# A pair's weighted sums, memory transposes and the second scores of the pair two later as one run of matmuls

## The chip, the cores and the metric

The kernel runs on one core of a Trainium2 chip. The metric is the device time of one execution in microseconds (us); of several executions the median counts. PE is TensorE, DVE VectorE, ACT ScalarE, POOL GpSimd, SP the engine that issues the loads.

## What is computed

An attention over 4 x 8 heads of 576 positions, 64 wide, with a recurrent memory mixed in, and two MLP layers on its output (512 to 2048 to 512 features, 2304 tokens):

```python
scores = scale * np.matmul(q, k.transpose(0, 1, 3, 2))
scores = np.where(causal, -1000000000.0, scores)
a = softmax(scores)
local = np.matmul(a, v)
q_p = phi(q)                      # elu(q) + 1
mem_out = einsum(q_p, M_prev) / (einsum(q_p, z_prev) + 1e-06)
x = g * mem_out + (1 - g) * local
h = x @ w_in;  x = (h * sigmoid(1.702 * h)) @ w_out          # layer 0
h = x @ w_in2; x = (h * clip(h + 3, 0, 6) / 6) @ w_out2      # layer 1
```

## The kernel before

**Tiles and pairs.** The tokens are cut into 6 tiles of 384. A tile needs the attention of one query block of 384 rows (g == 0) or of two blocks of 192 (g == 1), and the 8 heads of a block are handled as 4 pairs: 32 pairs, 4 of them for the first tile, then 4, 8, 4, 4 and 8. While the MLP's layer 0 runs on one tile, the attention of the next tile is worked in between its matmuls. Only the first tile's four pairs come before all MLP work (the opening). Layer 1 has no attention beside it.

**Steps of a pair.** `scores` multiplies q and k in two products (L545 to L560): the first, and the second, which for g == 0 is the last query rows and for g == 1 the remaining 64 rows of both heads. After each come a masked row minimum on DVE (L484), the exponential on ACT (L489), a reciprocal on DVE and the scaling on POOL (L497). `turn` transposes the probabilities on PE (L439) and copies them out of PSUM (L584 or L586). `mem_read` multiplies phi(q) with the memory (L409) and DVE scales the result (L680). `weigh` multiplies the transposed probabilities with v into one bank o, and adds the transposed memory output to it by matmuls with an identity (L704, L717, all recorded at L424); ACT copies o to the MLP's input (L735). A matmul in plain f32 stands in the trace as two records.

**Order.** The generator `attention` works on three pairs at a time (L756 to L777): the scores of pair i, the transposes of pair i - 1, the sums of pair i - 2. Its steps are: first scores, first transposes, sums, second scores, second transposes, and so on; each `yield` gives control back to the MLP's stream, and `pump` (L826) takes so many steps for each quarter of an MLP unit. A planner then orders each engine's instructions by its own estimate of times: those that are ready, earliest in program order first. `issue_after` (L340) keeps the MLP from running more than `SLACK` = 10 attention steps ahead.

**Runs.** `in_a_run` (L419) makes a matmul function of which each call must come after the one before it on PE, without a semaphore; only the first matmul waits, for the instructions in `deps`. The order is fixed by it, but not that nothing else may come between.

**Banks.** `bank` (L382) hands out PSUM banks in turn: 8 in the opening, then the three of `psa`, while the MLP has the other five. `free(t)` names the instruction that last read the bank that t takes over. The sums' run before is `in_a_run(list(made.pop(i).values()))`, where `made` has the copies of the transposes and the scaled memory output; the wait for the bank o is added by the framework. The second scores have a run of their own, `in_a_run(free(banks[0]) + free(banks[1]))`.

Of the kernel before, what the change touches and what calls it, by code (L numbers as in the profile page):

```python
# [104 lines left out]
def attention_moe_kernel(ctx: ExitStack, tc: tile.TileContext, qk0, sk0, sk1, vm0, vm1, bb, w1, w2, out):  # L105
# [271 lines left out]
    banks = [3, 0, 0]  # L377
# [22 lines left out]
    def free(t):  # L400

        d = last_read.get(place[id(t)][0])
        return [] if d is None else [d]

    on_pe = []
# [10 lines left out]
                reason="one run of matmuls",  # L416
            )

    def in_a_run(deps):  # L419

        run = []

        def mm(out, **args):
            ins = PE.matmul(out, **args).ins  # L424
            if run:
                tc.add_manual_dep(
                    ins, run[-1].name,
                    mybir.DependencyInfo(mybir.DependencyClass.NoSync, mybir.DependencyReason.DATA),
                    reason="one run of matmuls",
                )  # L430
            else:
                after(ins, deps)
            run.append(ins)
            on_pe[:] = [ins]

        return mm
# [4 lines left out]
    def attention(ap):  # L441
        qk, vm, pp, pt, phi, mo = {}, {}, {}, {}, {}, {}
        gens, made = {}, {}
        norms = [0, 0]

        t4 = ap.tile([128, 2, 64], F32, tag="t4", bufs=1, name="t4")
# [5 lines left out]
        def need(*keys):  # L452
            for key in keys:
                gen = gens.pop(key, None)
                if gen is not None:
                    chains.finish(gen)
# [45 lines left out]
        def scores(i):  # L502

            ti, si, b, g, p, _ = pairs[i]
            norms[1] = ti
            q, k = qk[i]
            st = ap.tile([128, 12], F32, tag="st", name="st")
            mx, su = st[:, 0:6], st[:, 6:12]

            def product(banks, blocks):  # L510

                mm = in_a_run(free(banks[0]) + free(banks[1]))
                for o0, o1, c0 in blocks:
                    for a in range(2):
                        h = slice(64 * a, 64 * a + 64)
                        mm(
                            banks[a][:, o0:o1], lhsT=q[h, c0:c0 + 128], rhs=k[h, 0:o1 - o0], start=True, stop=True
                        )

            def soft(s, cols, dst, c):  # L520

                jobs = [(a, c0, c1, c + a * len(cols) + x) for a in range(2) for x, (c0, c1) in enumerate(cols)]
                yield
                for a, c0, c1, k in jobs:
                    masked_min(s[a][:, c0:c1], mask[:, 512 - (c1 - c0):512], BIG, mx[:, k:k + 1])
                yield
                for a, c0, c1, k in jobs:
                    d = expo(dst[a][:, c0:c1], s[a][:, c0:c1], mx[:, k:k + 1], su[:, k:k + 1])
                    if c1 == cols[-1][1]:
                        has_read(s[a], d)  # L530
                yield
                inverse(su[:, c:c + len(jobs)])
                yield
                for a, c0, c1, k in jobs:
                    norm(dst[a][:, c0:c1], su[:, k:k + 1], omg[:, 2 * p + a:2 * p + a + 1])

            pp[i] = []
            if g == 0:
                parts = (((0, 128, 0), (128, 384, 128)), ((0, 384, 256),))
            else:  # L540
                parts = (((0, 512, 0),),)
            t = [[ap.tile([128, 512], F32, tag="p", bufs=PB, name="p") for _ in parts] for _ in range(2)]
            pp[i] = [tuple(x) for x in t]
            c = 0
            for x, blocks in enumerate(parts):  # L545
                s = [bank("s") for _ in range(2)]
                product(s, blocks)
                start(("s", i, x), soft(s, [(o0, o1) for o0, o1, _ in blocks], [t[a][x] for a in range(2)], c))
                c += 2 * len(blocks)
                yield  # L550
            if g == 1:
                t = ap.tile([128, 512], F32, tag="p", bufs=PB, name="p4")
                t2 = ap.tile([128, 64], F32, tag="p5", name="p5")
                pp[i].append((t, t2))
                s, s2 = bank("s4"), bank("s5")
                mm = in_a_run(free(s) + free(s2))
                for o, c0, c1 in ((s, 0, 512), (s2[:, 0:64], 512, 576)):
                    for a in range(2):
                        h = slice(64 * a, 64 * a + 64)
                        mm(o[h], lhsT=q[h, 128:N1], rhs=k[h, c0:c1], start=True, stop=True)  # L560

                def soft4(s=s, s2=s2, t=t, t2=t2):
                    yield
                    masked_min(s, mask[:, 0:1].to_broadcast([128, 512]), BIG, mx[:, 2:3])
                    masked_min(s2[:, 0:64], mask4, mx[:, 2:3], mx[:, 3:4])
                    yield
                    has_read(s, expo(t, s, mx[:, 3:4], su[:, 2:3]))
                    has_read(s2, expo(t2, s2[:, 0:64], mx[:, 3:4], su[:, 3:4]))
                    yield
                    DVE.tensor_tensor(out=su[:, 2:3], in0=su[:, 2:3], in1=su[:, 3:4], op=ALU.add)  # L570
                    inverse(su[:, 2:3])
                    yield
                    norm(t, su[:, 2:3], omp[:, p:p + 1])
                    norm(t2, su[:, 2:3], omp[:, p:p + 1])

                start(("s", i, 2), soft4())
                yield
# [114 lines left out]
        def weigh(i):  # L692

            ti, si, b, g, p, last = pairs[i]
            v = vm.pop(i)[0]
            t = pt.pop(i)
            need(("t", i, 0, 0), ("t", i, 0, 1), ("t", i, 1, 0), ("t", i, 1, 1), ("m", i))
            o = bank("o")
            mm = in_a_run(list(made.pop(i).values()))

            def av(j, rhs, c0, c1, first):
                for a in range(2):
# [33 lines left out]
                has_read(o, d)  # L736

            start(("x", i), split())
            yield

        def chunks(gen, n):
            for _ in range(n):
# [13 lines left out]
        for i in range(NPAIR + 2):  # L756
            if has(i):
                gs[i] = scores(i)
            if has(i - 1):
                gt[i - 1] = turn(i - 1)  # L760
            if has(i - 2):
                gw[i - 2] = weigh(i - 2)
            s, t, w = gs.pop(i, nil), gt.pop(i - 1, nil), gw.pop(i - 2, nil)
            for gen, n in (
                (s, 1), (t, 1), (w, 1), (s, 1), (t, 1), (w, 9), (s, 1), (t, 1), (s, 9),
            ):
                yield from chunks(gen, n)
            if has(i):
                start(("p", i), mem_prep(i))
                load_qk(i + 2)  # L770
            if has(i - 2) and pairs[i - 2][5]:
                need(("x", i - 2))
                yield pairs[i - 2][0]
            load_vm(i)
            if has(i - 1):
                yield from mem_read(i - 1)
            yield from chunks(t, 9)  # L777
# [180 lines left out]
```

## Time and profile before

| | us |
|---|---|
| median of 3 runs | 1064.96 (1061.93 to 1065.06) |
| profiled execution | 1062.62 |
| its span, first to last instruction | 1060.80 |
| mean granted TensorE clock | 0.995 |
| idle in the span: PE | 26.7 |

The page gives for each engine the busy time and its share of the span; the stretches give the same for parts of the span; the waits say who stood for whom; the timeline gives single instructions with their starts. Matmuls overlap, so the duration of one says less than the distance between two starts.

### The profile page before, as it was taken

To read this page: it belongs to the slowest core of one execution; us is meant where nothing else is said; L and a number is where in the kernel's file an instruction comes from. 1 tells how busy PE (TensorE), PEld (TensorE's weight loads), DVE (VectorE), ACT (ScalarE), POOL (GpSimd) and SP (SyncE) were. 2 spreads that over 40 slices of the span, in tenths; PEclk is the share of its full clock that TensorE was granted. 3 is DMA by queue.
4 is the path that set the end of the run, shared out by engine and by line. 5 is a ranking of instruction groups with operands and counts; after the bars stand their busy time and mean duration, and the time that the engine had idled before them with its cause. 6 is when DMAs were issued, how large, how long until landed. Compare 5 with 4: busy or idle time off the path is not lost.

```text
span 1060.8 us, 16126 instructions
## 1 busy us (share of the span) xinstructions
PE 1034.1 (97%) x6025; PEld 913.4 (86%) x6025; DVE 468.0 (44%) x1153; ACT 510.3 (48%) x1110; POOL 296.3 (28%) x346
## 2 busy tenths in 40 slices
PE   7899899999999999999999998999999999999998
PEld 4555456988788888888889998999999999999998
DVE  6975866666533333433344597881121111211210
ACT  5965745545544453433333677883233232332322
POOL 3511212323333232222322240432222222222221
PEclk9999999999999999999999999999999999999999
DMA  6753423332211111111100685001000010000000
GB/s 239 254 193 105 164 65 135 115 109 91 70 35 51 26 55 53 34 31 60 35 28 16 252 305 198 1 1 60 1 30 31 1 60 1 30 31 1 31 1 30
DMA packets 33886, 80.29 MB, mean 76 GB/s; under 512 B 4112, under 2 KB 13328, under 8 KB 33808
## 3 DMA queue, kind: packets, MB, share of 16 engines
q1 hardware_dynamic: 33808, 79.25, 22.3%
q8 instruction: 48, 0.79, 0.3%
q14 instruction: 30, 0.25, 0.1%
HBM read 61.41 MB, written 9.44 MB: 67 GB/s over the span
## 4 chain that ended last, share of the span: by engine, by line
PE 87%; ACT 5%; DVE 4%; DMA 3%; issue 1%; SPq 0%; POOL 0%; ACTq 0%; DVEq 0%; POOLq 0%
PE y L315 12%; PE y L317 11%; PE h L344 11%; PE y L316 11%; PE h L346 11%; PE h L347 11%; PE o L424 5%; PE s L424 5%; PE t L439 3%; PE y L313 2%; PE h L342 2%; ACT p L489 1%; PE mem L409 1%; DMA wt<-r 1%; ACT r L195 1%
## 5 line engine op out<-in xcount | busy, mean ns | idle before, releaser
L295 POOL TENSOR_TENSOR g<-t,g 128x384 fp32r<-128x384 f32 x173 | 186.5, 1079 | 482.1 <-ACT g L292 462.0
L344 PE MATMUL h<-xs,w 128*128 128x384 f32 x704 | 242.2, 344 | 6.0 <-DVE t L287 4.0
L315 PE MATMUL y<-g,w 128*128 128x384 f32 x704 | 237.6, 338 | 0.5 <-ACT g L292 0.5
L347 PE MATMUL h<-xs,w 128*128 128x384 f32 x704 | 236.7, 337 | 0.0
L316 PE MATMUL y<-g,w 128*128 128x384 f32 x704 | 236.6, 336 | 0.0
L346 PE MATMUL h<-xs,w 128*128 128x384 f32 x704 | 236.4, 336 | 0.0
L317 PE MATMUL y<-g,w 128*128 128x384 f32 x704 | 224.8, 338 | 0.0
L287 DVE SCALAR_TENSOR_TENSOR t<-t,h 128x384 f32<-128x384 f32 x96 | 53.1, 553 | 275.8 <-ACT t L285 275.6
L344 PEld LDWEIGHTS h<-xs,w 128*128 128x128 f32 x704 | 132.8, 189 | 13.9 <-issue 4.7
L497 POOL TENSOR_SCALAR p<-p,st,omg 128x128 f32<-128x128 f32 (+3 forms) x128 | 86.3, 686 | 199.8 <-DVE st L493 153.8
L285 ACT ACTIVATE t<-h,three 128x384 f32<-128x384 f32 x96 | 55.5, 579 | 173.4 <-PE h L347 172.1
L315 PEld LDWEIGHTS y<-g,w 128*128 128x128 f32 x704 | 132.2, 188 | 3.8 <-issue 1.0
L317 PEld LDWEIGHTS y<-g,w 128*128 128x128 f32 x704 | 130.5, 188 | 4.8 <-issue 4.1
L292 ACT CAST g<-t 128x384 fp32r<-128x384 f32 x176 | 90.1, 513 | 91.4 <-DVE t L287 49.3
L347 PEld LDWEIGHTS h<-xs,w 128*128 128x128 f32 x704 | 132.6, 188 | 0.5 <-issue 0.5
L346 PEld LDWEIGHTS h<-xs,w 128*128 128x128 f32 x704 | 132.9, 189 | 0.0
L316 PEld LDWEIGHTS y<-g,w 128*128 128x128 f32 x704 | 132.3, 188 | 0.5 <-issue 0.5
L489 ACT ACTIVATE p<-s,st 128x256 f32<-128x256 f32 (+4 forms) x160 | 82.4, 523 | 79.5 <-DVE st L484 63.5
L484 DVE CUSTOM_DVE_ANT_0 s<-s,mask 128x128 f32<-128x128 f32 (+3 forms) x144 | 72.2, 530 | 72.3 <-PE s L424 71.5
L281 ACT ACTIVATE t<-h 128x384 f32<-128x384 f32 x96 | 46.7, 489 | 73.0 <-PE h L347 54.3
L283 DVE SCALAR_TENSOR_TENSOR t<-t,h 128x384 f32<-128x384 f32 x80 | 44.0, 552 | 67.6 <-ACT t L281 60.5
L424 PE MATMUL s<-qk 64*128 64x256 f32 (+5 forms) x384 | 70.9, 460 | 2.2 <-ACT p L489 1.6
(82 smaller groups left out, 1110.5 us busy)
## 6 DMA issues: line engine op xcount, KB each, us to landing
r<-in_w_dram SPq DMA_DIRECT2D x64, 512.0 KB, 6.0
wt<-r SPq DMA_DIRECT2D x32, 256.0 KB, 2.4
vm<-in_vm_dram SPq DMA_DIRECT2D x16, 386.0 KB, 3.0
qk<-in_qk_dram SPq DMA_DIRECT2D x16, 384.0 KB, 3.7
qk<-in_sk_dram SPq DMA_DIRECT2D x32, 192.0 KB, 3.3
x2d<-yo SPq DMA_DIRECT2D x24, 192.0 KB, 2.0
xr<-x2d SPq DMA_DIRECT2D x24, 192.0 KB, 3.2
out_dram<-yo SPq DMA_DIRECT2D x24, 192.0 KB, 1.9
```

The source lines that it names most:

```text
L292: gated["ACT"].append(ACT.copy(out=g[:, 0], in_=t).ins)
L295: d = {"DVE": DVE, "POOL": POOL}[e].tensor_tensor(out=g[:, 1], in0=t, in1=f32(g[:, 0]), op=ALU.subtract)
L315: PE.matmul(ys[d], lhsT=w[:, 0, o:o + 128], rhs=g[:, 0], start=(f == 0), stop=False)
L316: PE.matmul(ys[d], lhsT=w[:, 1, o:o + 128], rhs=g[:, 0], start=False, stop=False)
L317: PE.matmul(ys[d], lhsT=w[:, 0, o:o + 128], rhs=g[:, 1], start=False, stop=(f == NF - 1))
L344: PE.matmul(h, lhsT=w[:, 0, c:c + 128], rhs=x[:, 0], start=first, stop=False)
L346: PE.matmul(h, lhsT=w[:, 1, c:c + 128], rhs=x[:, 0], start=False, stop=False)
L347: PE.matmul(h, lhsT=w[:, 0, c:c + 128], rhs=x[:, 1], start=False, stop=last)
L424: ins = PE.matmul(out, **args).ins
L484: DVE.tensor_tensor_reduce(out=o, in0=o, in1=m, scale=-SCALE, scalar=init, op0=ALU.add, op1=ALU.min, accum_out=out)
L489: return ACT.activation(out=dst, in_=o, func=AF.Exp, scale=-1.0, bias=m, accum_out=s)
L497: (DVE, POOL)[e[norms[0] % len(e)]].tensor_scalar(out=dst, in0=dst, scalar1=s, scalar2=w, op0=ALU.mult, op1=ALU.mult)
```

## The change

`weigh` now takes the two banks for the second scores of pair i + 2 first, and its own bank o after them; its first matmul waits for the copies, the memory output and the last readers of those two banks. It yields no longer in the middle: it leaves its last matmul in `tail`, and the second scores of pair i + 2, which are issued right behind it in the same step, take the two banks from `later` and put themselves behind `tail` without a wait of their own. One step with nothing in it (`yield None`) keeps the count of steps. The first scores are as before, as are the second scores of the first two pairs, and the sums of the last two pairs stand alone.

```diff
--- before.py
+++ after.py
@@ -416,9 +416,10 @@
                 reason="one run of matmuls",
             )
 
-    def in_a_run(deps):
-
-        run = []
+    def in_a_run(deps, run=()):
+
+
+        run = list(run)
 
         def mm(out, **args):
             ins = PE.matmul(out, **args).ins
@@ -441,6 +442,7 @@
     def attention(ap):
         qk, vm, pp, pt, phi, mo = {}, {}, {}, {}, {}, {}
         gens, made = {}, {}
+        later, tail = {}, []
         norms = [0, 0]
 
         t4 = ap.tile([128, 2, 64], F32, tag="t4", bufs=1, name="t4")
@@ -507,9 +509,17 @@
             st = ap.tile([128, 12], F32, tag="st", name="st")
             mx, su = st[:, 0:6], st[:, 6:12]
 
-            def product(banks, blocks):
-
-                mm = in_a_run(free(banks[0]) + free(banks[1]))
+            def two_banks(x):
+
+                s, run = later.pop((i, x), None), list(tail)
+                tail.clear()
+                if s is not None:
+                    return s, in_a_run([], run)
+                s = [bank("s") for _ in range(2)]
+                return s, in_a_run(free(s[0]) + free(s[1]))
+
+            def product(mm, banks, blocks):
+
                 for o0, o1, c0 in blocks:
                     for a in range(2):
                         h = slice(64 * a, 64 * a + 64)
@@ -543,8 +553,8 @@
             pp[i] = [tuple(x) for x in t]
             c = 0
             for x, blocks in enumerate(parts):
-                s = [bank("s") for _ in range(2)]
-                product(s, blocks)
+                s, mm = two_banks(x)
+                product(mm, s, blocks)
                 start(("s", i, x), soft(s, [(o0, o1) for o0, o1, _ in blocks], [t[a][x] for a in range(2)], c))
                 c += 2 * len(blocks)
                 yield
@@ -552,8 +562,7 @@
                 t = ap.tile([128, 512], F32, tag="p", bufs=PB, name="p4")
                 t2 = ap.tile([128, 64], F32, tag="p5", name="p5")
                 pp[i].append((t, t2))
-                s, s2 = bank("s4"), bank("s5")
-                mm = in_a_run(free(s) + free(s2))
+                (s, s2), mm = two_banks(1)
                 for o, c0, c1 in ((s, 0, 512), (s2[:, 0:64], 512, 576)):
                     for a in range(2):
                         h = slice(64 * a, 64 * a + 64)
@@ -692,11 +701,16 @@
         def weigh(i):
 
             ti, si, b, g, p, last = pairs[i]
+            yield from ()
             v = vm.pop(i)[0]
             t = pt.pop(i)
             need(("t", i, 0, 0), ("t", i, 0, 1), ("t", i, 1, 0), ("t", i, 1, 1), ("m", i))
+            deps = list(made.pop(i).values())
+            if has(i + 2):
+                later[i + 2, 1] = s = [bank("s") for _ in range(2)]
+                deps += free(s[0]) + free(s[1])
             o = bank("o")
-            mm = in_a_run(list(made.pop(i).values()))
+            mm = in_a_run(deps)
 
             def av(j, rhs, c0, c1, first):
                 for a in range(2):
@@ -736,7 +750,8 @@
                 has_read(o, d)
 
             start(("x", i), split())
-            yield
+            if has(i + 2):
+                tail[:] = on_pe
 
         def chunks(gen, n):
             for _ in range(n):
@@ -761,10 +776,16 @@
             if has(i - 2):
                 gw[i - 2] = weigh(i - 2)
             s, t, w = gs.pop(i, nil), gt.pop(i - 1, nil), gw.pop(i - 2, nil)
-            for gen, n in (
-                (s, 1), (t, 1), (w, 1), (s, 1), (t, 1), (w, 9), (s, 1), (t, 1), (s, 9),
-            ):
-                yield from chunks(gen, n)
+            yield from chunks(s, 1)
+            yield from chunks(t, 1)
+            for _ in w:
+                pass
+            if has(i - 2):
+                yield from chunks(s, 1)
+                yield None
+            yield from chunks(s, 1)
+            yield from chunks(t, 1)
+            yield from chunks(s, 9)
             if has(i):
                 start(("p", i), mem_prep(i))
                 load_qk(i + 2)
```

## Rows read from the trace of the kernel before

**Rows 1.** The page, part 1: busy us (share of the span) x instructions
```profile
PE 1034.1 (97%) x6025; PEld 913.4 (86%) x6025; DVE 468.0 (44%) x1153; ACT 510.3 (48%) x1110; POOL 296.3 (28%) x346
```

**Rows 2.** Stretches: length, busy us of each engine, granted clock, DMA share, GB/s
```profile
46.00:152.00 106.00, 100.35 (x417) 57.66 (x417) 75.32 (x158) 65.80 (x118) 25.60 (x26) 0.98 0.42 143
152.00:586.00 434.00, 429.54 (x2704) 366.31 (x2701) 200.19 (x619) 197.45 (x522) 128.83 (x166) 1.00 0.20 61
```

**Rows 3.** Waits of PE: who for whom, us in total, times, longest
```profile
PE o L424 <- ACT p L489: 2.6, 2, 2.1
```

**Rows 4.** PE's timeline at two pairs: start us, us, engine line op out<-in shape xcount
```profile
220.59 0.33 PE L316 MATMUL y<-g,w 128*128 128x384 f32 x1
...
221.28 0.34 PE L317 MATMUL y<-g,w 128*128 128x384 f32 x1
221.55 1.52 PE L424 MATMUL o<-pt,vm 128*64 128x192 f32 x16
...
223.49 1.19 PE L424 MATMUL s<-qk 64*64 64x512 f32 x8
...
224.89 0.34 PE L316 MATMUL y<-g,w 128*128 128x384 f32 x1
...
543.64 0.34 PE L315 MATMUL y<-g,w 128*128 128x384 f32 x1
543.90 1.52 PE L424 MATMUL o<-pt,vm 128*64 128x192 f32 x16
...
545.92 0.34 PE L317 MATMUL y<-g,w 128*128 128x384 f32 x1
...
546.27 0.34 PE L316 MATMUL y<-g,w 128*128 128x384 f32 x1
547.94 0.34 PE L344 MATMUL h<-xs,w 128*128 128x384 f32 x1
```

**Rows 5.** PE's timeline at a pair that was cut
```profile
483.34 0.34 PE L347 MATMUL h<-xs,w 128*128 128x384 f32 x1
483.61 1.19 PE L424 MATMUL o<-pt,vm 128*64 128x192 f32 x10
...
494.04 1.18 PE L424 MATMUL s<-qk 64*64 64x512 f32 x6
...
495.82 0.34 PE L346 MATMUL h<-xs,w 128*128 128x384 f32 x1
```

**Rows 6.** Timeline of all engines at three pairs; in brackets idle before and releaser
```profile
122.46 2.17 PE L424 MATMUL o<-pt,vm 128*64 128x384 f32 x12 [2.12 <-ACT p L489]
...
123.41 0.70 ACT L489 ACTIVATE p<-s,st 128x512 f32<-128x512 f32 x1
123.60 0.68 DVE L586 COPY pt<-t 128x512 f32<-128x512 f32 x1
...
198.98 1.52 PE L424 MATMUL o<-pt,vm 128*64 128x192 f32 x16
...
200.70 0.68 DVE L586 COPY pt<-t 128x512 f32<-128x512 f32 x1
...
237.38 1.52 PE L424 MATMUL o<-pt,vm 128*64 128x192 f32 x16 [0.50 <-ACT p L489]
237.60 0.69 ACT L489 ACTIVATE p<-s,st 128x512 f32<-128x512 f32 x1
```

**Rows 7.** PE's timeline in the opening
```profile
25.66 0.92 PE L424 MATMUL s<-qk 64*128 64x384 f32 x4
...
28.83 1.52 PE L424 MATMUL o<-pt,vm 128*64 128x384 f32 x12 [0.37 <-DVE mo L680]
...
44.28 0.94 PE L409 MATMUL mem<-vm,phi 128*128 128x130 f32 x6 [1.05 <-ACT p L489]
...
46.35 0.91 PE L342 MATMUL h<-x,r 128*128 128x384 f32 x2 [0.20 <-ACT pt L584]
```

**Rows 8.** A stretch around the stand at 122 us, columns as in the second group
```profile
122.00:128.00 6.00, 5.54 (x22) 3.36 (x23) 5.93 (x10) 2.68 (x6) 2.11 (x2) 0.72 0.31 98
```

## The prediction

> **What bounds the kernel now.** I read the page's busy line first, then the stretches, then TensorE's (PE's) waits, then its timeline around single pairs. PE is busy 1034.1 of 1060.8 us [rows 1], so time is saved only by taking work or idle time off PE. The change touches the attention, which PE runs up to 586 us, between the MLP's matmuls. By stretches PE stands idle 5.65 us from 46 to 152 us and 4.46 us from 152 to 586 us (length less busy time) [rows 2]. In the waits, the weighted sums stand for softmax exponentials 2.6 us in all, 2 times, the longest 2.1 [rows 3]. So waits in front of these sums are rare now, and idle time is no large store to win from. What is left is what it costs PE to turn from MLP matmuls to attention matmuls and back.
>
> **What a joined run saves.** There are 30 pairs whose sums are followed by scores of a later pair; 4 of them lie in the opening (before 46 us) and 26 later. First the step of the MLP's stream: four starts from 220.59 to 221.28 us, 0.173 us each [rows 4]. I price a visit to the attention by starts: from the start of the last MLP matmul before it to the second start after it, less two steps of 0.173 (the second, since the first one after a visit is drawn out). Apart, at 543.90 us: the 20 sums with their 2 transposes take 545.92 - 543.64 - 0.35 = 1.93 us, the 8 second scores 547.94 - 546.27 - 0.35 = 1.32 us, together 3.25 us. Joined, at 221.55 us, sums, transposes and scores in one go: 224.89 - 221.28 - 0.35 = 3.26 us [rows 4]. So a joined visit costs the same as two. PE already ran them joined in 21 of the 26 later pairs (the one of 221.55 among them), and the other 5 would gain nothing by it. Saved: 5 x -0.01 to 0.01 us, **0.0 us**.
>
> **What cuts cost, and whether the change mends them.** The links between a run's matmuls fix their order and no more: an MLP matmul may still be put between two of them. At 483.61 us the sums were cut after 10 of 20, and the scores ended at 494.04 with the 6 left over. From 483.34 to 495.82 us are 12.48 us; in them lie 38 MLP starts (6.57 us) and the 4 transposes of another product (0.44 us), which leaves 5.5 us for what costs 3.26 us uncut: 2.2 us lost [rows 5]. One other pair, of 174.62 us, is cut in its scores, by my reading of the same timeline for about 1.3 us, what the first piece of two matmuls costs alone (as many as eight cost together). So cuts that touch these runs cost 3.5 us. The scores are now issued one step earlier, together with the sums, and stand ahead of more MLP matmuls; that speaks for fewer cuts. But the sums were linked before too, and were cut. Bounds: -3.5 us (all mended) to +3 us (as many new ones); I take **-1.0 us**, a bit nearer to none, since the cause (an MLP matmul that comes due in mid-run) is not removed.
>
> **What the joined wait costs.** Before, the first sum waits for the evacuated transposes, the scaled memory output and one bank: of three attention banks it reuses the one that the first score product's first head left. The second scores wait, behind 1.9 us of sums, for the second head's exponential and for the evacuation of the transposes issued just before. After, the scores take their two banks first and the sums the third, and all of it is waited for in front of the first sum: both exponentials and that evacuation. A waiting sum holds the whole in-order PE, the MLP matmuls behind it, and through them the gates on ScalarE and VectorE. I go by each pair's rows and ask when the latest of the three was done. In 20 of the 26 later pairs all were done before the sums began; cost nothing, hidden by the MLP matmuls in front. Two pairs are the dear ones because PE already stands there: at 122.46 us the sums begin 0.15 us after one exponential, while the second ends at 124.11 and the copy at 124.28: 1.8 us more; at 237.38 us the second exponential ends at 238.29: 0.9 us more [rows 6]. In the other four the copy ends about when the sums begin or up to 2.4 us after it (the longest: sums at 198.98, copy done at 201.38 [rows 6]); there PE was not standing, MLP matmuls came next, and the scheduler, which places a run when its estimate says that it is ready, can put them in front. So between 0 (all covered) and 1.8 + 0.9 + 2.4 + 0.4 + 0.2 = 5.7 us (none covered); I take **+1.5 us**, about half of the two sure ones, since matmuls of the MLP follow them also. What comes next is later too: the next transposes now reuse a bank of the second scores and wait for its exponential, where they waited for the copy of the sums. Between visits lie MLP matmuls that cover it, as with the 20 pairs: 0, and where that cover is gone it is part of the slower rival.
>
> **The opening.** Here no MLP matmul covers anything. The second scores of pair 3 ran at 25.66 us, ahead of the sums of pair 1 at 28.83, which waited 0.37 us for the memory output [rows 7]. Bound to come after these sums, their 0.85 us leave a stretch in which PE idles anyway and move into one in which it runs densely: +0.85 us. Those of pairs 4 and 5 likewise change places with sums, inside dense work: 0 each. Against that, VectorE has one 0.55 us score mask less ahead of that memory output: down to -0.5 us. At the end, the memory product at 44.28 us waits 1.05 us for an exponential of pair 5's second scores, and the first MLP matmul follows at 46.35 us [rows 7]; with these scores later that wait may grow by the 1.5 us of the sums that now come first, or vanish, since the first MLP matmul can be put ahead. From -0.5 to +2.4 us; I take **+0.9 us**. The softmax of the second scores starts one step earlier, and nothing else moves: SP's loads and POOL's scaling keep their places in the generators' order.
>
> **Sum.** 0.0 - 1.0 + 1.5 + 0.9 = +1.4 us. The profiled execution took 1062.62 us (span 1060.80), so by itself 1064.0; the median of the three runs, 1064.96, is 2.3 us above it, so I forecast 1064.96 + 1.4 = **1066 us**, which is no change.
>
> **The rivals.**
> *Slower: the joined wait stands uncovered.* Place: the first sum of a pair. Price: 5.7 us of waits. To it comes the clock: from 122 to 128 us, after PE had stood 2.1 us and twice about 1 us before, the granted clock was 0.72 on average [rows 8], between its levels of 2.4 and 1.2 GHz; 6 x 0.28 = 1.7 us lost. With the opening's 0.9 and no mended cut that is +8.3 us: 1073 us. It decides from 3.2 us of new standing in front of the sums. For it: the two pairs of [rows 6]. Against it: the 20 pairs that have slack. The Trainium skill, "TensorE: Matmul & The Clock Gate", section "HAM oscillation — how this bites in real kernels", says that waits between bursts throttle the clock, so that the next burst runs cold; the trace agrees at 122 us (0.72) and nowhere else between 46 and 586 us. By that rule, one more such stand would cost another 1.7 us.
>
> *Faster: the cuts go, and so does the stand at 122 us.* Mended cuts give -3.5 us; a new order in which MLP matmuls stand before those sums gives the 2.1 us of waiting and the 1.7 us of clock back; -7.3 us at most, and with the opening's 0.9 about 1059 us, half of it 1062. For it: earlier scores, and a schedule that is made anew throughout. Against it: nothing in the change points at 122 us in particular, where it adds a wait.
>
> *It doesn't do what it says.* The run is only linked, and gets cut between sums and scores as before. A cut between the transposes and the scores costs nothing (1.93 + 1.32 against 3.26); one inside costs about 1.3 us. With four of these more, less the gain taken, it is 1064.96 + 0.9 + 1.5 + 3 = 1070 us; with none, the forecast.
>
> **How the numbers follow.** About 0.3% (3.2 us) is what a measurement of this kernel can tell from no change. Forecast 0.42 (within); slower by the uncovered wait 0.24; faster 0.26; cut as before 0.08, half of it within and half slower. So faster 0.26, within 0.46, slower 0.28. Cases of both signs hold more than half, so the forecast's own range stands apart: 1062 to 1069 us. The range of all reaches to the middle of the faster rival and to most of the slower one: 1059.5 to 1072 us.
>
> **What would show it.** Right: sums, transposes and scores without an MLP matmul between them in nearly all pairs, and a visit at 3.25 us; the span within 3 us. The waits of the sums for exponentials and copies then come to 3 to 5 us against 2.6 [rows 3]. The slower rival would show as such waits of over 6 us, or as a second stretch with the clock under 1; the faster one as idle time from 46 to 586 us well under 10.1 us, or no cut run. The opening is read off the first MLP matmul: 46.35 us now, 47.2 by the forecast. I am wrong in mechanism if a joined visit costs clearly less than 3.25 us, or if the time moves beyond 586 us, where nothing was changed.

## The result and the profile after

| | before | after |
|---|---|---|
| median (range) of five executions each, us | 1063.42 (1061.93 to 1065.06) | 1071.21 (1069.53 to 1074.77) |
| profiled execution, us | 1062.62 | 1069.53 |
| its span, us | 1060.8 | 1067.7 |

The changed kernel is slower by 0.8%: the ratio of the times is 1.0080, 95% interval 1.0065 to 1.0095. The time lies inside the stated range of 1059.5 to 1072 us, close to the upper end that the slower rival had set; the forecast itself, no change, did not come true.

First the page's busy line of the changed kernel, to be held against [rows 1]:

```profile
PE 1035.9 (97%) x6025; PEld 916.7 (86%) x6025; DVE 466.0 (44%) x1153; ACT 510.0 (48%) x1110; POOL 294.0 (28%) x346
```

The instructions are the same in number. PE is busy 1.8 us longer in a span that is 6.9 us longer, so it also stands idle 5 us more. The stretches (columns as in [rows 2]) say where:

```profile
0.00:46.00 46.00, 35.58 (x212) 23.40 (x214) 34.41 (x134) 32.41 (x101) 20.46 (x43) 0.93 0.64 229
46.00:152.00 106.00, 97.08 (x406) 55.61 (x402) 71.33 (x156) 66.97 (x120) 23.35 (x26) 0.97 0.41 143
152.00:586.00 434.00, 428.93 (x2688) 364.79 (x2685) 203.86 (x624) 197.95 (x528) 128.76 (x167) 1.00 0.19 61
```

From 46 to 152 us the idle time went from 5.65 to 106.00 - 97.08 = 8.92 us; from 152 to 586 us from 4.46 to 5.07 us. For a full account I split the span of the profiled executions into three parts: time in which no matmul record lies (idle), busy time times one less the granted clock (clock), and the rest, which is the work at full clock. Before: 26.8 + 5.1 + 1029.0. After: 31.8 + 8.9 + 1027.0. So 5.1 us more idle, 3.8 us more at the low clock, and 2.0 us less work. These are single executions; the changed kernel's is the fastest of its five.

The start of the first matmul of a tile gives the loss by place:

| profiled execution, us | first MLP matmul | second tile | sixth tile | end of span |
|---|---|---|---|---|
| before | 46.4 | 169.8 | 580.5 | 1060.8 |
| after | 42.7 | 176.7 | 587.0 | 1067.7 |

The changed kernel is 6.9 us late at the second tile, 6.5 us late at the sixth, and 6.9 us at the end. So the loss is there by the time the attention of the first 170 us is done. By the second tile both kernels have the same matmuls behind them, the sums of nine pairs among them, so the stretch from there to the sixth tile compares like with like: 410.8 us before and 410.3 after, with 1.6 us more idle time and 2.1 us less work.

PE's waits (engine, line, for whom; us in total, times, longest) of after, those that answer to [rows 3]:

```profile
PE s L425 <- ACT p L491: 5.4, 3, 2.0
PE mem L409 <- ACT p L491: 4.5, 4, 1.5
PE h L342 <- DVE r L206: 3.6, 1, 3.6
PE o L425 <- ACT p L491: 2.6, 2, 2.0
```

The sums' own waits for exponentials (the last line) are 2.6 us, as before. What grew stands in front of other work: first scores (s), memory products (mem), and one MLP matmul (h) that waits for a converted weight.

The largest of these stands, in the timeline of DVE and PE:

```profile
120.56 0.29 DVE L486 CUSTOM_DVE_ANT_0 s<-s,mask,st 128x64 f32<-128x64 f32 x1
...
120.77 0.69 DVE L186 TENSOR_SCALAR r<-r 128x1024 int32<-128x1024 int32 x1
...
123.92 1.22 PE L425 MATMUL s<-qk 64*128 64x512 f32 x4 [1.20 <-ACT pt L593]
...
128.06 1.22 DVE L206 SCALAR_TENSOR_TENSOR r<-r 128x1024 f32<-128x1024 f32 x1
...
129.33 2.93 PE L342 MATMUL h<-x,r 128*128 128x384 f32 x4 [3.61 <-DVE r L206]
```

and the stretch that begins in it (columns as in [rows 2]; the granted clock is ahead of the last two):

```profile
128.00:134.00 6.00, 4.67 (x8) 2.52 (x8) 3.52 (x8) 2.42 (x5) 1.51 (x2) 0.50 0.53 164
```

The MLP matmul at 129.33 us needs a weight whose conversion starts on DVE at 120.77 us, right behind the masks of second scores, and those are now behind the sums. It ends at 129.28 us, PE stands 3.61 us, and the granted clock from 128 to 134 us is 0.50, the lower of its two levels.

In the opening, PE's timeline, to be held against [rows 7]:

```profile
32.34 1.65 PE L425 MATMUL s<-qk 64*128 64x128 f32 x8 [1.87 <-ACT p L491]
...
41.39 0.93 PE L425 MATMUL s<-qk 64*128 64x128 f32 x8 [1.48 <-ACT p L491]
42.25 0.44 PE L440 MATMUL t<-ident,p 128*128 128x128 f32 x2
42.69 2.20 PE L342 MATMUL h<-x,r 128*128 128x384 f32 x6
44.82 1.41 PE L425 MATMUL o<-pt,vm 128*64 128x384 f32 x10
```

The first scores of pairs 4 and 5 stand 1.87 and 1.48 us for exponentials: by the order in which banks are handed out they take a bank of the second scores of pairs 3 and 4, and those run later now. The first MLP matmuls moved ahead of pair 3's sums, to 42.69 us.

### The profile page after: what moved, and what is told of

It is laid out like the page before. It is cut to its first block, busy times and chain, and to the rows that moved or that the text cites. A ratio compares the mean times of both kernels' runs of the same rounds, so it can differ in the third digit from the quotient of the medians.

```text
span 1067.7 us, 16107 instructions
## 1 busy us (share of the span) xinstructions
PE 1035.9 (97%) x6025; PEld 916.7 (86%) x6025; DVE 466.0 (44%) x1153; ACT 510.0 (48%) x1110; POOL 294.0 (28%) x346
## 4 chain that ended last, share of the span: by engine, by line
PE 89%; ACT 4%; DVE 4%; DMA 2%; issue 1%; SPq 0%; DVEq 0%; ACTq 0%
PE y L315 11%; PE h L344 11%; PE y L316 11%; PE y L317 11%; PE h L346 11%; PE h L347 11%; PE o L425 5%; PE s L425 5%; PE h L342 4%; PE y L313 3%; PE t L440 3%; ACT p L491 2%; PE mem L409 1%; DVE s L486 1%; DVE r L186 1%
## 5 line engine op out<-in xcount | busy, mean ns | idle before, releaser
L486 DVE CUSTOM_DVE_ANT_0 s<-s,mask 128x128 f32<-128x128 f32 (+2 forms) x144 | 72.3, 529 | 79.4 <-PE s L425 78.5
```

What stands on the lines that cost most here:

```text
L486: DVE.tensor_tensor_reduce(out=o, in0=o, in1=m, scale=-SCALE, scalar=init, op0=ALU.add, op1=ALU.min, accum_out=out)
```

## The experiments

Each was timed beside the kernel before on the same chip; that kernel's median was 1062.7 us in the first four runs that follow (e1 to e4), 1063.28 in the next four, and 1063.2 in the last four. Differences between two of these kernels are given below as differences of medians; by their ratios to the kernel before they come out within 0.7 us of that.

### Which half: the opening or the rest

**e1_late** joins from pair 4 on alone; **e2_opening** in pairs 0 to 3 alone. The edit is the same condition with the two signs:

```diff
-            if has(i + 2):
+            if joins(i):
                 later[i + 2, 1] = s = [bank("s") for _ in range(2)]
...
+        def joins(i):
+            return has(i + 2) and i >= 4
```

> Joined runs only from pair 6's second scores on (the sums of pairs 4 and later); the opening is as before. Theory O (opening): the whole loss comes from the opening, where sums and scores change places and banks, and from what follows from it up to 170 us; then the first MLP matmul starts at 46.4 us as before, no MLP matmul stands for a converted weight (3.6 us at 129 us in the changed kernel), tile 1 begins at 170 and the time is 1063 to 1065 us. Theory W (wait): the loss comes from the joined waits in front of the later pairs' sums; 26 of 30 joined runs are still there, so 1070 to 1072 us.

> The other half: joined runs only for the four sums of the opening (pairs 0 to 3), all later ones as before. Theory O: 1069 to 1072 us, tile 1 begins 6 to 7 us later than before (170). Theory W: 1063 to 1065 us. If both halves give about half of the 8 us, both hold.

Measured: e1_late 1069.52 us (1069.11 to 1071.19), ratio 1.0061 [1.0043, 1.0080]; e2_opening 1065.06 us (1062.63 to 1068.26), ratio 1.0022 [1.0008, 1.0036]. The two add up to 0.83%, the whole 0.80%. So about 2.4 us come from the opening and the larger part, some 6.8 us, from the pairs worked in between MLP matmuls. (e1_late is half a microsecond under theory W's range, e2_opening at the top of it. Theory O is out, though one of its signs holds for e1_late too: an MLP matmul stands for a converted weight, 2.22 us at 100 us.)

### The order of the banks

**e3_obank** is the changed kernel with the sums' bank taken first again:

```diff
+            o = bank("o")
             if has(i + 2):
                 later[i + 2, 1] = s = [bank("s") for _ in range(2)]
                 deps += free(s[0]) + free(s[1])
-            o = bank("o")
```

**e7_swapbanks** is the kernel before with that order alone changed, and no run joined:

```diff
+            if has(i + 2):
+                later[i + 2, 1] = [bank("s") for _ in range(2)]
             o = bank("o")
```

> The changed kernel with one thing undone: the sums take their bank first and the second scores the next two, as before; the runs stay joined, and the first sum still waits for all three. Theory O by banks: in the opening the first scores of pairs 4 and 5 no longer take over a bank of the second scores just before them (they stood 1.9 and 1.5 us for its exponential), so half or more of the 8 us comes back: 1064 to 1067 us. Theory O by order (the second scores stand behind the sums whatever the bank): 1069 to 1072. Theory W: the waits are the same three, 1070 to 1072 us.

> The kernel before with one thing changed: the second scores' two banks are taken ahead of the sums' bank. Undoing the banks' order in the changed kernel gave nothing (1071.0), so 1061 to 1065 us; if the order costs by itself in the opening (first scores that take over a bank of second scores), 1065 to 1067.

Measured: e3_obank 1070.97 us, ratio 1.0069 [1.0048, 1.0090], not apart from the changed kernel; e7_swapbanks 1062.38 us, ratio 0.9986 [0.9976, 0.9996], a hair faster. The order of the banks is not the cause. Nor do the two stands of the opening show what the opening costs: in e3_obank the longest in front of those first scores is 0.92 us, another of 3.07 us came in front of transposes at 43.86 us, and the time stayed.

### The wait in front of the sums

**e4_ownwait** is the changed kernel, with the run tied as it is, but the second scores wait for their banks at their own first matmul. **e5_lateown** is e1_late with the same edit.

```diff
                 if s is not None:
-                    return s, in_a_run([], run)
+                    return s, in_a_run(free(s[0]) + free(s[1]), run)
...
-                later[i + 2, 1] = s = [bank("s") for _ in range(2)]
-                deps += free(s[0]) + free(s[1])
+                later[i + 2, 1] = [bank("s") for _ in range(2)]
```

> The changed kernel, but the second scores wait for their two banks at their own first matmul, not at the first sum; order, link and banks as changed. Theory W: the price is the wait in front, so 1063 to 1066 us. Theory O: 1069 to 1072 us, with the stand for a converted weight near 129 us still there.

> Both halves of the loss undone at once: linked runs only from the sums of pair 4 on, and the second scores wait at their own first matmul; what stays is the link and the banks' order. If the joined wait costs about 5 us (1071.2 against 1065.9 without it) and the opening about 2.4 (the opening alone gave 1065.1 against 1062.7), then 1062 to 1064 us, as before the change. If the link itself costs (it puts the scores one step earlier and behind the sums), 1066 to 1068. If it helps by fewer cuts, under 1061.

Measured: e4_ownwait 1065.88 us (1063.15 to 1068.13), ratio 1.0024 [1.0011, 1.0038]; e5_lateown 1064.71 us, ratio 1.0015 [1.0005, 1.0026]. The wait in front of the sums is worth 1071.21 - 1065.88 = 5.3 us in the one pair of kernels and 1069.52 - 1064.71 = 4.8 us in the other. e5_lateown fell between its two ranges and stays 1.4 us above the kernel before. Rows of the wait, in the changed kernel first (ACT and PE around the sums at 290 us):

```profile
288.71 0.47 ACT L593 COPY pt<-t 128x384 f32<-128x384 f32 x1
...
289.42 0.49 ACT L491 ACTIVATE p<-s,st 128x256 f32<-128x256 f32 x1
...
290.05 1.52 PE L425 MATMUL o<-pt,vm 128*64 128x192 f32 x16 [1.96 <-ACT p L491]
```

and the same pair in e4_ownwait:

```profile
287.19 0.47 ACT L593 COPY pt<-t 128x384 f32<-128x384 f32 x1
287.35 1.52 PE L425 MATMUL o<-pt,vm 128*64 128x192 f32 x16 [0.78 <-ACT p L491]
...
287.90 0.49 ACT L491 ACTIVATE p<-s,st 128x256 f32<-128x256 f32 x1
```

In e4 the sums start before the second head's exponential, at 287.90 us, has begun: they stand 0.78 us and are released when the first head's is done. In the changed kernel the sums start when that second exponential is over (289.42 + 0.49 = 289.91), and PE has stood 1.96 us. The sums don't read it; it is the last reader of a bank that the second scores take. Two more such stands fall away, 0.69 us at 259 us and, in front of a memory product, 0.89 us at 543 us. That is 1.18 + 0.69 + 0.89 = 2.8 us that the rows show; the rest of the 5 us lies in the clock and in the order of other work, which was laid out anew.

Not every stand in front of sums goes with the wait. The longest in e4_ownwait is one of them, near the place where the changed kernel's MLP matmul stood for its weight:

```profile
131.02 1.52 PE L425 MATMUL o<-pt,vm 128*64 128x384 f32 x12 [2.97 <-ACT p L491]
```

By place, e4_ownwait is no earlier than the changed kernel at the second tile (179.4 against 176.7 us, with one more pair's sums behind it), and 3.6 us earlier at the sixth (583.4 against 587.0).

**e6_waitalone** and **e12_swapwait** put the same wait into the kernel before without tying the runs, e6 with the sums' bank taken first and e12 with the second scores' banks taken first:

```diff
-            mm = in_a_run(list(made.pop(i).values()))
+            deps = list(made.pop(i).values())
+            if has(i + 2):
+                later[i + 2, 1] = s = [bank("s") for _ in range(2)]
+                deps += free(s[0]) + free(s[1])
+            mm = in_a_run(deps)
```

> The kernel before with one thing added: the sums' first matmul waits for the readers of the two banks of the second scores as well. No link, no other bank order, the scores are issued in their own step. The wait as the cause of the larger part: 1066 to 1069 us, with stands of 1 to 2 us in front of sums. The wait only harmful together with the link and the step: within 3 us of 1062.7.

> The kernel before, with the banks of the second scores taken ahead of the bank of the sums, and the sums waiting for those banks, but the sums and the second scores not tied into one run. The wait alone gave 1064.5 us against 1063.2, the order of the banks alone 1062.4. If the wait costs only where nothing may stand between sums and scores, this gives 1061.5 to 1065 us; if the wait and the changed order of the banks together make the stands of the changed kernel, 1067 to 1071 us.

Measured: e6_waitalone 1064.50 us, ratio 1.0013 [1.0004, 1.0023]; e12_swapwait 1066.66 us (1064.04 to 1067.26), ratio 1.0025 [1.0014, 1.0035]. e12 fell between what the two theories gave. Against e7_swapbanks, which differs from it in the wait alone, it is 4.3 us slower; e6 against the kernel before is 1.2 us slower, with 3.0 us more idle time and 3.2 us less work in its account. The profiled execution of e6 also has 2.3 us more of the low clock. So the wait costs something by itself, with no run joined, but e6 is in the range of the theory that it harms only together with the link and the step. A row in e12 is of the kind above:

```profile
240.11 0.69 DVE L586 COPY pt<-t 128x512 f32<-128x512 f32 x1
...
240.68 0.69 ACT L489 ACTIVATE p<-s,st 128x512 f32<-128x512 f32 x1
...
241.52 1.52 PE L424 MATMUL o<-pt,vm 128*64 128x192 f32 x16 [1.55 <-ACT p L489]
```

but its longest stand is in front of an MLP matmul that waits for a gate of the MLP on DVE, at the place where in the kernel before the sums stood 2.12 us:

```profile
125.70 5.49 PE L342 MATMUL h<-x,r 128*128 128x384 f32 x8 [3.38 <-DVE g L283]
```

In the accounts of the profiled executions e12 has 2.3 us more idle time than e7, 4.8 us more of the low clock and 2.7 us less work.

### The converted weight at 129 us

**e8_weights_earlier** loads the weights of the MLP's layer 0 two blocks further ahead of their conversion. **e11_unpin** no longer holds the first operation of a conversion in program order on DVE.

```diff
-AHEAD = 2
+AHEAD = 4
```
```diff
-PIN = (True, False)
+PIN = (False, False)
```

> The changed kernel with the raw weights of layer 0 loaded four tiles ahead instead of two, so that they stand in front of a value load that the sums hold back on the load queue. If the stand of 3.6 us for a converted weight at 129 us is a loss of its own, caused by late loads: 1066 to 1069 us and that stand gone. If PE would stand for the attention there anyway, or the conversions are late for VectorE and ScalarE rather than for the load: 1070 to 1072.

> The changed kernel, but the first operation of each conversion of a weight to the MLP's form is not held in program order on VectorE. If the stand of 3.6 us in front of the MLP's matmul near 129 us, and the slow clock behind it, come from that operation standing on VectorE behind the masks of the second scores, the stand falls below 1 us and the time by 3 to 5 us, to 1066 to 1068 us. If that stand only takes the place of idle time that would come anyway, it goes and the time stays at 1070 to 1072 us.

Measured: e8_weights_earlier 1071.55 us, ratio 1.0076 [1.0056, 1.0095], with the same stand of 3.61 us at 129.6 us: it is not the loads. e11_unpin 1071.75 us, ratio 1.0079 [1.0049, 1.0109]: the stand at 129 us is gone, another of 2.25 us in front of a converted weight came at 145.8 us, and the time is the same. Its first MLP matmul starts at 55.4 us, 12.7 us later than in the changed kernel, for the planner laid out the opening anew; so the run shows that this stand can be moved without a gain, and not what it costs in its place.

### The empty step

The changed kernel keeps the count of steps by an empty one behind the second scores. **e9_stepfirst** has it in front of the sums; **e10_latestep** is e1_late with the same edit.

```diff
+            if has(i - 2):
+                yield None
             for _ in w:
                 pass
             if has(i - 2):
                 yield from chunks(s, 1)
-                yield None
```

> The changed kernel with one thing moved: the empty step of the order of TensorE (in which other work is placed) stands in front of a pair's sums instead of behind the second scores. If the loss is that the joined wait stands uncovered (the sums wait for the exponentials whose banks the scores take, 1.96 us at 290 us and 0.89 us at 543 us in the changed kernel), the work placed in that step hides it: no stand above 1 us in front of sums behind ACT's exponentials after 200 us, and a median of 1065 to 1068 us against about 1071. If the loss lies in the opening or in the stand in front of a converted weight near 129 us, those stay and so does the time, 1070 us or more.

> The kernel with joined runs from pair 4 on alone (opening as before), and in front of each joined sum an empty step for other work. By the theory of the uncovered wait both the opening's 2.4 us and the stands in front of sums go: 1062 to 1065 us against 1069.5 for the same kernel with the step behind the scores, within 0.2% of the kernel before. If the longer link between sums and scores costs by itself, whatever stands in front, 1066 to 1069 us.

Measured: e9_stepfirst 1065.91 us (1063.15 to 1069.01), ratio 1.0028 [1.0013, 1.0042], 5.3 us under the changed kernel; e10_latestep 1063.22 us (1061.89 to 1064.99), ratio 0.9999 [0.9988, 1.0009], 6.3 us under e1_late and equal to the kernel before. The times came as the theory of the uncovered wait said; its rows did not. The stand of 1.96 us in front of the sums is in both (289.6 and 283.9 us), and so are stands of 0.89 us in front of memory products. e9 even has one of 4.73 us in front of sums, at 136.9 us. (Its profiled execution, 1069.01 us, is the slowest of its ten, so that its trace and the changed kernel's don't show the 5.3 us.) By place:

| from one start to the next, us | to the first MLP matmul | to the second tile | to the sixth tile |
|---|---|---|---|
| before | 46.4 | 123.4 | 410.8 |
| e1_late (wait in front, step behind) | 46.1 | 128.8 | 413.1 |
| e5_lateown (own wait, step behind) | 46.4 | 127.4 | 407.4 |
| e10_latestep (wait in front, step in front) | 46.1 | 122.8 | 411.3 |

All four have the same opening, and the sums of nine pairs behind them at the second tile; e10 has four records of scores and four of transposes less there, which take 1.6 us in e1 (from 127.29 to 128.85 us). The table separates two costs. The place of the step is worth 128.8 - 122.8 = 6.0 us in the first tile, 1.6 of which are this work put off, and 1.8 us behind it. The place of the wait is worth 413.1 - 407.4 = 5.7 us from the second tile to the sixth, and only 1.4 us in the first. Half of the 5.7 us are the stands named above (the idle time there falls from 4.5 to 1.7 us), the other half 2.9 us of low clock that one execution has and the other has not. These are single executions, and e1's is the slowest of its four; the medians of the kernels differ by 6.3 and 4.8 us. Against the kernel before, the joined run with its own wait is 4.0 us slower in the first tile and 3.4 us faster from the second to the sixth: what the wait in front costs there is in part a gain that it takes away.

The 6.0 us of the first tile are, in the account, 2.1 us of idle time (8.9 to 6.8), 1.4 us of low clock (4.8 to 3.4) and 2.5 us of work (115.1 to 112.6). Up to the sixth tile the difference is 7.8 us: 2.0 of idle time, 4.4 of low clock and 1.4 of work. How the idle time differs can be seen early in it. The stretch from 46 to 100 us of e1_late:

```profile
46.00:100.00 54.00, 50.18 (x209) 29.24 (x209) 37.48 (x80) 33.46 (x64) 13.76 (x15) 0.99 0.57 193
```

its PE near the end of that stretch:

```profile
96.61 1.13 PE L425 MATMUL s<-qk 64*128 64x512 f32 x4 [1.92 <-ACT pt L593]
97.67 0.55 PE L440 MATMUL t<-ident,p 128*128 128x128 f32 x3
100.44 5.43 PE L342 MATMUL h<-x,r 128*128 128x384 f32 x8 [2.22 <-DVE r L206]
```

the same stretch of e10_latestep:

```profile
46.00:100.00 54.00, 53.76 (x218) 31.57 (x218) 37.00 (x78) 32.57 (x63) 13.99 (x15) 1.00 0.56 193
```

and its PE at the same scores:

```profile
97.53 2.75 PE L313 MATMUL y<-g,r 128*128 128x384 f32 x8
100.21 1.13 PE L425 MATMUL s<-qk 64*128 64x512 f32 x4
101.27 0.55 PE L440 MATMUL t<-ident,p 128*128 128x128 f32 x3
104.83 2.80 PE L342 MATMUL h<-x,r 128*128 128x384 f32 x5 [3.01 <-DVE r L206]
```

In e10 eight MLP records lie right in front of the scores, and their 1.92 us of standing are gone. In e1 they come behind the scores: another eight (L342), which e10 ran at 91.05 us, stand there for a converted weight until 100.44 us, and the MLP is 16 records behind. That weight's conversion on DVE, first and last operation, in e1_late:

```profile
92.20 0.69 DVE L186 TENSOR_SCALAR r<-r 128x1024 int32<-128x1024 int32 x1
...
99.16 1.22 DVE L206 SCALAR_TENSOR_TENSOR r<-r 128x1024 f32<-128x1024 f32 x1
```

and in e10_latestep:

```profile
83.74 0.73 DVE L186 TENSOR_SCALAR r<-r 128x1024 int32<-128x1024 int32 x1
...
88.41 1.23 DVE L206 SCALAR_TENSOR_TENSOR r<-r 128x1024 f32<-128x1024 f32 x1 [1.00 <-ACT r L201]
```

So with the step in front the conversion began 8.5 us earlier. Idle time from 46 to 100 us is 0.24 us against 3.82, of which the next stretch, to 175 us, gives 1.5 us back. In this tile PE stands for converted weights in both kernels (2.22 and 3.01 us), so MLP matmuls are scarce there, and the steps of the attention set where they are spent. Why the planner puts that conversion later with the step behind is not shown.

## Why the prediction came out as it did

**What bounds the kernel**: as said. PE is the bound, its idle time and its clock decide, and nothing changed beyond the sixth tile: 480.3 us from its start to the end before, 480.7 after.

**What a joined run saves, 0.0 us**: right. In the changed kernel, PE's timeline at one pair:

```profile
224.80 0.34 PE L317 MATMUL y<-g,w 128*128 128x384 f32 x1
225.07 1.52 PE L425 MATMUL o<-pt,vm 128*64 128x192 f32 x16
...
228.12 0.44 PE L344 MATMUL h<-xs,w 128*128 128x384 f32 x1
228.40 0.34 PE L346 MATMUL h<-xs,w 128*128 128x384 f32 x1
```

A visit costs 228.40 - 224.80 - 0.35 = 3.25 us, as in [rows 4]. And it does what it says: 22 of the 26 later runs are in one piece. That rival is out. (By the order of PE's starts 19 were in one piece before, and 22 had nothing between sums and scores; the prediction's count of 21 was a little off, and it missed a cut in front of the two transposes at 464.20 us.)

**Cuts, -1.0 us**: right in sign. The cuts that touched these runs in [rows 5] are gone from their places, and others came: in the sums at 205.2, 472.3 and 496.1 us after 14 of 20, and one run in four pieces from 181.6 us. The work at full clock is 2.0 us less, all changes of hands taken together, inside the bounds of -3.5 to +3; how much of it is cuts is not shown.

**The joined wait, +1.5 us**: this is the term that was mis-sized. The runs with the wait moved to the scores give 5.3 and 4.8 us, near the upper bound of 5.7; by the rows 2.8 us of it are stands. The sentence that failed is that the scheduler can put MLP matmuls in front of such a run: at 290 us nothing was put there in 1.96 us. (Perhaps its estimate had the run ready by then; no run shows the estimate.) And the two pairs that I called dear in [rows 6] are not where it was lost. I had read each pair's slack from the places that the pairs have in the kernel before, and the planner gave each of them a new place; the stand of 2.12 us at 122 us is gone, and others came at 259, 290 and 543 us.

**The opening, +0.9 us**: also too small. e2_opening gives +2.4 us, the upper bound, and by the table below that is low clock: the rest of its span is no longer than before. Its mark, the first MLP matmul at 47.2 us, was wrong in sign: it came at 42.69, put ahead of sums, so it says nothing of the cost. What I missed is that the first scores of pairs 4 and 5 take banks of the second scores that now come later (1.87 and 1.48 us); but e3_obank, without these two stands, took the same time, so they don't explain the loss.

**The empty step** had no term. I had written that one step keeps the count, and not that its place, behind the scores and no longer between the sums and them, decides where MLP matmuls go. With the step behind, the second scores come one step earlier than before and the sums keep theirs; with it in front, the scores keep theirs and the sums come one later. Moving it in front is worth 5.3 and 6.3 us. Together with the 5 us of the wait that is more than the 7.8 us lost: either the two overlap, or both edits together would come out under the kernel before.

**The clock**: I had 1.7 us for one more stretch at the low level, in the slower rival alone. The changed kernel's profiled execution lost 3.8 us more to it than that of the kernel before: 2.6 us up to the sixth tile, and 1.2 us in layer 1, where nothing was changed (below). Every execution has its span and its mean granted clock on record, so this can be told from all of them. Here are, as means, the share that was not granted times the span, and what is left of the span. The former counts idle time too; in the profiled executions of these kernels that makes it 0.1 to 1.9 us too high. (One execution of the kernel before, of 1699.6 us, is left out.)

| kernel (executions) | span, us | not granted, us | the rest, us |
|---|---|---|---|
| before (68, beside e1 to e12) | 1061.5 | 7.4 | 1054.1 |
| changed (5) | 1070.1 | 12.4 | 1057.7 |
| e1_late (4) | 1068.0 | 13.9 | 1054.1 |
| e2_opening (10) | 1063.1 | 11.0 | 1052.2 |
| e4_ownwait (10) | 1064.2 | 11.1 | 1053.2 |
| e5_lateown (10) | 1063.1 | 11.7 | 1051.4 |
| e9_stepfirst (10) | 1064.0 | 9.7 | 1054.3 |
| e10_latestep (10) | 1061.3 | 8.7 | 1052.6 |

So about half of what the changed kernel lost is low clock, and most of what each half lost alone. Moving the step in front takes e1_late's time at the low clock down by 5.2 us of the 6.7; for the wait, and for the step in e9, the share of the clock (1.3 to 2.7 us) is not clear of that error. The sum of the prediction left the clock out. That the place of the wait and of the step decide the time is shown by the runs that move them; which stand brings how much of the low clock is not shown.

**The rivals.** The slower one was right in its cause, the joined wait, and in the second stretch under clock 1 that it named (0.50 from 128 to 134 us). It was wrong in its place: it said that the sums' waits would pass 6 us, and they are 2.6 us as before. The time went to first scores, memory products and a converted weight, that is, to what the new order of the steps put behind. The faster rival had one thing right, that the stand at 122 us would go; it went, and others took its place.

**The sum**: +1.4 us was forecast, +6.9 us is the difference of the profiled executions, +7.8 us that of the medians. With the wait at 5 and the opening at 2.4 instead of 1.5 and 0.9, and the rest as it was, the sum of the prediction would have been 0.0 - 1.0 + 5 + 2.4 = +6.4 us, the slower rival's side. That this comes near is in part luck: it has no term for the step and none for the clock, and the 5 us are measured against a joined run with its own wait, not against the kernel before.

**What stays open**: why nothing was put in front of the sums at 290 us, and what the stand at 129 us costs in the changed kernel's own order. The step in front together with the scores' own wait, which by the table should keep the gains of both places, was not tried. Of what was run, e7_swapbanks (1062.38 us) and e10_latestep (1063.22 us) are no more than 0.14% from the kernel before.

## What to carry to other kernels

To put a later consumer's waits in front of an earlier one saves nothing by itself on an in-order engine that switches at the same price joined or apart; it moves the wait to where less can cover it, so price it at its upper bound unless the rows show what stands ready to be put in front. Where a planner lays out the whole program anew, slack read pair by pair from the old trace is no bound: take the largest stand as a price, and count how many places could have it. And count the steps of a hand-written order as part of the change: an empty step on the other side of a run was worth as much here as the wait itself. Then look at the granted clock of all executions before explaining a loss by the stands of one: here it held about half.

## What the runs showed of the hardware

The same stand is followed by a slow clock in one kernel and not in another. The 1.96 us in front of the sums at 290 us are in the changed kernel, e1_late, e3_obank, e8, e9, e10 and e11, between 1.958 and 1.964 us long. Behind it the granted clock (the column ahead of the last two) was 1.00 in the changed kernel:

```profile
290.10:293.40 3.30, 3.30 (x31) 2.37 (x31) 0.75 (x3) 0.83 (x2) 1.94 (x4) 1.00 0.16 36
```

and 0.50 in e1_late:

```profile
290.10:293.40 3.30, 3.30 (x20) 2.01 (x16) 0.00 (x0) 0.83 (x2) 1.77 (x4) 0.50 0.19 26
```

where PE's timeline has sixteen records of the sums in 2.25 us and not 1.52:

```profile
289.35 2.25 PE L425 MATMUL o<-pt,vm 128*64 128x192 f32 x16 [1.96 <-ACT p L491]
```

In e9 it was 0.50 too, in the remaining four 1.00. The Trainium skill, "TensorE: Matmul & The Clock Gate", section "HAM oscillation — how this bites in real kernels", tells of a kernel whose waits for DMA between bursts of matmuls let the clock fall, so that the next burst starts cold. Stands of about 2 us, for another engine, did so here in two kernels and not in five. In layer 1, which the change doesn't touch, the stand of 4.0 us is in every kernel, and behind it the clock was low for half of a stretch in the kernel before:

```profile
662.50:669.30 6.80, 6.71 (x30) 6.71 (x31) 3.36 (x6) 5.47 (x9) 3.95 (x3) 0.75 0.00 0
```

and for the whole of it in the changed one:

```profile
667.30:674.10 6.80, 5.77 (x18) 5.77 (x19) 3.67 (x5) 5.47 (x10) 3.94 (x3) 0.50 0.05 17
```

In the account that is 2.9 us of low clock in layer 1 against 1.7. So two executions may differ by over a microsecond at one such place, in code that is the same; a difference of this size between single executions need not have a cause in the change.
